# A pre-norm block with linear attention and an MLP: attention weights turned by DMA from DRAM, key folds by 128 rows, and a new hand-written order ahead of the MLP

## The chip, the cores and the metric

The kernel runs on one core of a Trainium2 chip. A core has five engines that run side by side, each with its own queue of instructions: TensorE (PE in the profile; PEld is its weight load), VectorE (DVE), ScalarE (ACT), GpSimd (POOL) and SyncE (SP), which here only issues DMAs. They wait for each other through semaphores. The metric is the device time of one execution in microseconds (us), as the median of several runs.

## What is computed

The reference, cut to what matters (x is 2048 tokens by D = 576, 32 heads of 18, F = 4608, all in bf16):

```python
def attention(x, wqkv, w_phi, wo):
    q, k, v = split(x @ wqkv)                     # 32 heads of 18
    pq, pk = q @ w_phi[head], k @ w_phi[head]
    phi = lambda p: concat(softmax(p), softmax(-p))
    kv = phi(pk).T @ v ; z = phi(pk).sum(tokens)
    o = (phi(pq) @ kv) / (phi(pq) @ z + 1e-6)
    return o @ wo
h   = x + attention(layernorm(x), ...)
y   = layernorm(layernorm(h))                     # one by the block, one by the MLP
out = h + gelu(y @ w1 + b1) @ w2 + b2
```

## The kernel before, in words

**Tiles.** The 2048 tokens lie in 16 tiles of 128, handled as 8 pairs p = 0 to 7 (a = 0 or 1 is the tile in the pair). `xh` holds x. D is cut into 9 chunks of 64. A normalised pair (`lnb`, three buffers in turn) is transposed into `lnT` so that partitions 0 to 63 hold a chunk of tile a = 0 and 64 to 127 the same chunk of tile a = 1. A projection (`project`, L420) is then 18 matmuls of 64 rows, two at a time on the two halves of TensorE, 9 chunks deep; every weight must therefore lie on both halves of the partitions.

**Attention weights.** The feature matrix `w_phi` is folded into the key and query weights once: `spread` (L215) lays `w_phi` out as a block diagonal `bd`, and a fold multiplies turned weights by it. For the keys, `load_wk` (L153) loads them in three DMAs, `flip_mm` (L361) turns them by 25 transposes on TensorE, `flip_ev` (L369) copies them out of PSUM, and `fold_k_mm` (L376) folds one chunk of 64 rows twice, once for either half of the partitions (10 matmuls, 9 chunks, 90 in all); `fold_k_ev` (L388) is the copy out of PSUM into `wkp`, all nine on ACT. For the queries, `load_wq` (L597) makes five DMAs in pieces of 252 bytes, `turn_wq` (L373) turns them by five DMAs from SBUF to SBUF, and five `fold_mm("q", c)` fold 128 rows each; `swap_q` (L409) copies halves across, so that query projections already read crossed slots of their weights (`CROSSED`, L418). The value weights are loaded to partitions 0 to 63 by two DMAs (`load_values`, L163) and copied to 64 to 127 by four GpSimd copies (`copy_values`, L171).

**Work of a pair.** `stats` (L287, VectorE), `power` (L298, GpSimd: variance to the power of -1/2), `centre` and `scale` (L305, L308: the normalised tile, on the engine named in the call), then the turning: `turn_x_mm` on TensorE for pairs 0 and 1, `turn_dma` (L320, issued by SP) for the others. Then for either half i of the heads `value_mm` and `key_mm` (TensorE into PSUM), `value_ev` (copy), `key_exp` (two exponentials on ACT), `key_sum` (L491: sum and reciprocal, VectorE), `key_weigh` (L494: the product with the reciprocal, one call for each a, all on GpSimd) and `sums(p, a)` (L554: 11 matmuls that gather phi(k) times v over all tokens in `acc_kv`). Queries: `query_mm`, `query_exp`, then `query_sum`, `query_weigh` and `turn_q` (a DMA transpose) when the pair's output is due. When all 16 `sums` are done, `table` (L569) takes `acc_kv` into `kvm`; `combine_mm`, `divide`, `turn_o_mm`, `residual_mm`, `residual_add`, `residual_stats`, `second`, `rescale` and `turn2_mm` carry pair 0 to the MLP's input, and the first matmul of the MLP is L1150. The MLP (`up` L1137, `down` L1178) runs over blocks of 256 or 512 tokens; attention outputs of later pairs are worked in between.

**Order.** The order on all engines is the order in which the calls stand (a manual schedule); L771 to L1116 are a list of some 340 calls, from `warm(13)` (TensorE matmuls on the identity) to `gelu_table()`. An engine takes its own instructions in that order and waits at each for what it needs. PSUM for this stage is three buffers of two banks (`two`), handed out in turn, and `pn`. The turned weights, `bd` and `wph` are borrowed from the space of the first quarter of the MLP's first weights (`borrowed`, L123), so `load_w1(0, n)` waits for the last fold that reads there; `load_w1(1, n)` waits until keys and values are given up (`close_keys`, L619).

## Time and profile before

| | us |
|---|---|
| median of 3 runs | 392.42 (392.41 to 392.46) |
| span of the profiled execution | 391.0 |
| first key fold on TensorE | 9.61 |
| first projection | 15.82 |
| first `combine_mm` | 71.03 |
| first matmul of the MLP | 85.26 |

The profile shows one execution. Its span runs from the first to the last instruction, and the runs' median lies 1.4 us above it. Rows of the timeline give start, duration, engine, line, operation, output <- inputs, shapes and count. Rows by line give busy time in us, the mean of one in ns, and the idle time ahead of them with what ended it. Rows by windows give a stretch and its length, then the busy time (and count) of PE, PEld, DVE, ACT and POOL, the granted TensorE clock, the share of the DMA engines and their GB/s. In a DMA row, "to landing" is the time from issue to the last byte.

### The profile page before, as it was taken

The page shows a single profiled execution, that of the slowest core. Times are in us where ns is not written, and L with a number is a line of the kernel's source. Part 1 is how long each engine was busy: PE and PEld are TensorE (multiplying, and loading weights), DVE is VectorE, ACT ScalarE, POOL GpSimd, SP SyncE. Part 2 cuts the span into 40 slices and gives each one's busy share as a digit, 9 for nine tenths or more (in the row PEclk, how much of TensorE's full clock was granted, in tenths as well). Part 3 has the DMA queues.
Part 4 walks back from the last instruction along what each step waited for, and adds up shares of the span by engine and source line. Part 5 has one row for each costly group of instructions (what it writes and reads, how often), then busy time and mean ns, then how long its engine had stood idle before and what let it go on. Part 6 is the DMA issues. An engine that isn't in the chain of part 4 may idle for free.

```text
span 391.0 us, 10251 instructions
## 1 busy us (share of the span) xinstructions
PE 383.6 (98%) x4492; PEld 267.2 (68%) x4493; DVE 163.5 (42%) x367; ACT 163.7 (42%) x290; POOL 128.2 (33%) x167
## 2 busy tenths in 40 slices
PE   8899999999999999999999999999999999999997
PEld 4687777779878887844457887444677764447773
DVE  6989894595249388590029322000480000000100
ACT  3978887678501850056650000666300026661000
POOL 8899999214604564144003111000031110000120
PEclk9999999999999999999999999999999999999999
DMA  8999749999655666643005542000041000000000
GB/s 220 189 182 175 163 98 184 227 300 254 206 106 104 95 107 134 107 61 62 0 2 63 90 106 48 16 1 2 2 102 50 17 17 0 2 2 0 17 29 18
DMA packets 76108, 34.76 MB, mean 89 GB/s; under 512 B 63026, under 2 KB 73536, under 8 KB 76064
## 3 DMA queue, kind: packets, MB, share of 16 engines
q1 hardware_dynamic: 75376, 32.47, 41.9%
q0 software_dynamic: 400, 1.35, 1.3%
q8 instruction: 35, 0.57, 0.6%
q10 hardware_dynamic: 288, 0.30, 0.3%
q14 instruction: 9, 0.07, 0.1%
HBM read 16.53 MB, written 2.36 MB: 48 GB/s over the span
## 4 chain that ended last, share of the span: by engine, by line
PE 94%; DVE 4%; POOL 1%; issue 1%; POOLq 0%
PE po L1194 36%; PE ph L1150 36%; PE pk L426 7%; PE pa L697 5%; PE pv L426 4%; PE acc_kv L562 2%; PE pw L250 1%; PE pn L648 1%; DVE st L293 1%; POOL wv L174 1%; DVE ob L662 0%; PE pW L396 0%; DVE shared L260 0%; PE pT L338 0%; DVE shared L314 0%
## 5 line engine op out<-in xcount | busy, mean ns | idle before, releaser
L1172 ACT ACTIVATE home<-ph,b1col 128x512 bf16<-128x512 f32 (+1 forms) x180 | 98.5, 598 | 169.6 <-PE ph L1150 166.3
L1194 PE MATMUL po<-w,home 128*128 128x288 bf16 (+2 forms) x1151 | 143.3, 286 | 0.1
L1150 PE MATMUL ph<-shared,w 64*128 64x512 bf16 (+2 forms) x1638 | 141.3, 332 | 0.1
L1194 PEld LDWEIGHTS <-home 128*128 128x128 bf16 x1152 | 109.2, 98 | 32.3 <-issue 1.8
L1150 PEld LDWEIGHTS <-w 64*128 64x128 bf16 x1638 | 80.3, 94 | 60.0 <-issue 1.0
L1198 DVE TENSOR_TENSOR ot<-po,hb 128x288 bf16<-128x288 f32 (+2 forms) x32 | 14.5, 454 | 106.5 <-PE po L1194 100.7
L1183 POOL TENSOR_TENSOR hb<-xh,b2bc 128x576 f32<-128x576 bf16 x16 | 20.4, 1272 | 104.6 <-DVE ot L1198 95.2
L426 PEld LDWEIGHTS <-home 64*128 64x128 bf16 x864 | 42.0, 94 | 10.8 <-issue 1.1
L512 POOL TENSOR_TENSOR padded<-home,rq 128x540 bf16<-128x540 bf16 x32 | 34.8, 1101 | 36.4 <-DVE rq L504 14.9
L256 POOL TENSOR_TENSOR rs<-va,mhalf 128x1 f32<-128x1 f32 x16 | 8.8, 550 | 105.0 <-DVE va L254 105.0
L706 DVE TENSOR_TENSOR xh<-pa,xh 128x288 bf16<-128x288 f32 x32 | 13.2, 449 | 71.6 <-PE pa L697 71.6
L483 POOL TENSOR_TENSOR phik<-phik,rk 128x576 bf16<-128x576 bf16 x32 | 36.4, 1164 | 1.4 <-PE pv L426 0.9
L477 DVE TENSOR_REDUCE sk<-phik 128x64 f32<-128x1152 bf16 x16 | 21.2, 1327 | 5.4 <-ACT phik L448 5.4
L448 ACT ACTIVATE home<-pk 128x576 bf16<-128x576 f32 x32 | 18.9, 649 | 6.9 <-PE pk L426 5.7
L503 DVE TENSOR_REDUCE sk<-home 128x64 f32<-128x1152 bf16 x16 | 21.0, 1313 | 0.0
L426 PE MATMUL pv<-wv,home 64*128 64x288 bf16 x288 | 20.9, 283 | 0.1
L426 PE MATMUL pk<-wqp,home 64*128 64x288 bf16 x288 | 20.0, 283 | 0.2 <-ACT home L448 0.2
L448 ACT ACTIVATE phik<-pk 128x576 bf16<-128x576 f32 x32 | 18.7, 652 | 3.1 <-PE pk L426 3.1
L426 PE MATMUL pk<-shared,home 64*128 64x288 bf16 x288 | 19.9, 283 | 0.0
L661 DVE RECIPROCAL rec<-pn 128x18 f32<-128x18 f32 (+1 forms) x32 | 8.0, 250 | 27.9 <-PE pn L648 27.9
L697 PE MATMUL pa<-wo,shared 64*128 64x288 bf16 x288 | 18.8, 283 | 0.0
L697 PEld LDWEIGHTS <-shared 64*128 64x128 bf16 x288 | 13.9, 94 | 4.3 <-issue 0.5
(78 smaller groups left out, 209.0 us busy)
## 6 DMA issues: line engine op xcount, KB each, us to landing
w<-in_B_w_dram SPq DMA_DIRECT2D x21, 432.0 KB, 7.0
out_dram<-ot SPq DMA_DIRECT2D x15, 144.0 KB, 1.9
xh<-in_A_x_dram SPq DMA_DIRECT2D x3, 576.0 KB, 7.3
wo<-in_A_wo_dram SPq DMA_DIRECT2D x4, 324.0 KB, 6.3
w<-in_B_w_dram POOLq DMA_DIRECT2D x3, 432.0 KB, 10.5
wv<-in_A_wqkv_dram SPq DMA_DIRECT2D x2, 324.0 KB, 9.9
w<-in_A_wqkv_dram SPq DMA_DIRECT2D x4, 157.5 KB, 8.7
wqp<-wqp SPq DMA_DIRECT2D x2, 288.0 KB, 3.9
```

Source lines behind the costliest of these rows:

```text
L426: nc.tensor.matmul(dst[:, a, 0:HALF], lhs[rows, c, :], w[rows, slot, i * HALF : (i + 1) * HALF], start=(n == 0), stop=(n == KC - 1),)
L448: nc.scalar.activation(rows[:, :, i * HH : (i + 1) * HH, s, :], flight[key, p, i][:, :, 0:HALF].rearrange("p a (h f) -> p a h f", f=DH), A ...
L477: nc.vector.tensor_reduce(sk[:, :, :], part_of(dst, i), AX.X, ALU.add)
L483: eng.tensor_tensor(part, part, flight["r" + key, p, i][:, a, :].rearrange("p (h o) -> p h o", o=1).to_broadcast([P, NH, DH]), ALU.mult,)
L503: nc.vector.tensor_reduce(sk[:, :, :], part_of(phiq[p], i), AX.X, ALU.add)
L512: eng.tensor_tensor(padded[:, a, g0 * P : (g0 + 5) * P].rearrange("p (g k) -> p g k", k=P)[:, :, 0:STEP].rearrange("p g (h f) -> p g h f", ...
L697: nc.tensor.matmul(pa[a], oT[p % 2][rows, c, :], wo[rows, c, cs], start=(c == 0), stop=(c == KC - 1),)
L1150: nc.tensor.matmul(ph[half][:, lo:hi], w1[p_ // 9][rows, c, p_ % 9 * P : (p_ % 9 + 1) * P], ln2T[rows, c, base + lo : base + hi], start=(c ...
L1172: nc.scalar.activation(hidden(m), ph[half][:, 0:width], AF.Gelu_apprx_tanh, bias=b1col[:, m : m + 1], scale=1.0,)
L1183: nc.gpsimd.tensor_tensor(hb[:, :], xh[:, t, :], b2bc[:, :], ALU.add)
L1194: nc.tensor.matmul(po[:, :], hidden(m)[:, i_ * P : (i_ + 1) * P], w2[m // 18][:, m % 18, cs], start=(j == 0), stop=(j == NM - 1),)
L1198: nc.vector.tensor_tensor(ot[:, cs], po[:, :], hb[:, cs], ALU.add)
```

## The change

- **Key and query weights** are turned by DMA straight from DRAM: ten `dma_start_transpose` of 576 rows by 128 columns (pieces of 256 bytes), five for the keys ahead of everything else on SP behind one load of x, five for the queries later in the order. `load_wk`, `flip_mm`, `flip_ev`, `load_wq` and the memsets of padding go.
- **Key folds** take 128 rows at once: 5 matmuls instead of 10 (the ninth still has 10). The weights then lie in slots that hold two neighbouring chunks, one on either half, so keys and values are read crossed like the queries (`WINDOWS`).
- **Value weights** come by four DMAs, whole rows, loaded for both halves; no copy on GpSimd.
- **x** is loaded in larger parts, the first parts from ACT's queue; tiles 12 to 15 ahead of 8 to 11.
- **b1** is turned by a DMA instead of a TensorE transpose.
- **Engines:** 8 of 16 `scale` calls are on GpSimd (none before), 4 on ACT (8 before), 4 on VectorE (8 before); 10 of 32 `key_weigh` and 1 of 4 `query_weigh` on VectorE (none before); 3 of 9 `fold_k_ev` on VectorE; one of the two last `turn2_ev` on ACT. Some memsets change between VectorE and GpSimd. Small tiles have other numbers of buffers.
- **Order:** a new list of calls; `load_w1(1, n)` is issued inside `close_keys`, still by SP and GpSimd in turn.

The diff of the helpers, cut:

```diff
+    def turn_weights(dst, at, g):
+        nc.sync.dma_start_transpose(
+            dst[:, g, :], A_wqkv[:, at + g * 126 : at + g * 126 + P]
+        )
+    def turn_wk(g):
+        turn_weights(wTk, D, g)
+    def turn_wq(g):
+        turn_weights(wTq, 0, g)
+    def load_values(part, eng):
+        if part < 2:
+            eng.dma_start(
+                wv[:, 4 * part : 4 * part + 4, :],
+                A_wqkv[part * KH : part * KH + 512, 2 * D : 3 * D].rearrange(
+                    "(c p) f -> p c f", p=P
+                ),
+            )
+            return
+        r0 = 512 if part == 2 else 0
+        eng.dma_start(
+            wv[(part - 2) * KH : (part - 1) * KH, 8, :], A_wqkv[r0 : r0 + KH, 2 * D : 3 * D]
+        )
...
+    load_x(0, 1, nc.scalar)
+    load_x(1, 2, nc.sync)
+    load_x(2, 4, nc.scalar)
+    load_x(4, 8, nc.scalar)
+    for g in range(NG):
+        turn_wk(g)
...
-    def fold_k_mm(c):
-        flight["k", c] = two.tile([P, 2, 512], FP32, name="pW", tag="two")[:, :, :]
+    def fold_k_mm(n):
+        flight["k", n] = two.tile([P, 2, 512], FP32, name="pW", tag="two")[:, :, :]
+        if n < 8:
+            f0 = n // 4 * KH + n % 4 * P
+            parts = [(slice(0, P), slice(f0, f0 + P))]
+        else:
+            parts = [(slice(0, KH), slice(512, D)), (slice(KH, P), slice(0, KH))]
         for g in range(NG):
             k = P if g < NG - 1 else 72
-            for a in range(2):
+            for rows, fs in parts:
                 nc.tensor.matmul(
-                    folded_part(g, "k", c, slice(a * KH, (a + 1) * KH)),
-                    wT[:k, g, c * KH : (c + 1) * KH],
+                    folded_part(g, "k", n, rows), wTk[:k, g, fs],
...
-    PLAIN = [(c, c) for c in range(KC)]
+    WINDOWS = [(n, (2 * n, 2 * n + 1)) for n in range(4)]
+    WINDOWS += [(4 + n, (2 * n + 1, 2 * n + 2)) for n in range(4)] + [(8, (8, 0))]
```

The new order as a whole (the list before has the same kinds of calls, with the differences named above), calls in a row:

```python
    warm(12); load_values(0, syn); stats(0, 0); load_values(1, pool); stats(0, 1); load_values(3, syn); power(0); centre(0, 0); stats(1, 0);
    scale(0, 1, vec); stats(1, 1); load_values(2, syn); spread(3); spread(4); stats(2, 0); scale(0, 0, act); spread(1); turn_x_mm(0); load_b1();
    spread(2); spread(0); load_x(12, 16, syn); power(1); turn_x_ev(0, 0, act); fold_k_mm(2); turn_x_ev(0, 1, act); fold_k_mm(1); fold_k_ev(1, act);
    fold_k_mm(4); fold_k_ev(2, dve); fold_k_mm(3); fold_k_mm(0); scale(1, 0, vec); fold_k_ev(3, dve); fold_k_ev(4, act); scale(1, 1, pool);
    load_x(8, 12, syn); fold_k_mm(6); stats(2, 1); fold_k_ev(0, act); turn_x_mm(1); fold_k_ev(6, act); fold_k_mm(7); turn_x_ev(1, 1, act);
    turn_x_ev(1, 0, dve); fold_k_ev(7, dve); fold_k_mm(8); turn_wq(3); power(2); stats(3, 0); fold_k_ev(8, act); stats(3, 1); fold_k_mm(5);
    value_mm(0, 1); fold_k_ev(5, act); stats(6, 0); turn_wq(1); key_mm(1, 0); centre(2, 1); power(3); value_mm(1, 1); scale(2, 0, pool); stats(6, 1);
    value_ev(0, 1, act); key_exp(1, 0); scale(2, 1, act); stats(4, 0); centre(3, 1); value_mm(1, 0); value_ev(1, 1, act); key_mm(0, 0);
    value_mm(0, 0); power(6); stats(4, 1); turn_wq(2); key_exp(0, 0); value_ev(1, 0, dve); value_ev(0, 0, act); turn_dma(2); scale(3, 1, act);
    stats(5, 0); scale(3, 0, pool); key_mm(0, 1); stats(5, 1); power(4); scale(4, 1, pool); key_sum(0, 0); value_mm(2, 0); turn_dma(3);
    key_exp(0, 1); power(5); key_sum(1, 0); key_sum(0, 1); key_mm(2, 1); key_mm(2, 0); value_ev(2, 0, act); key_weigh(0, 0, 1, pool);
    scale(5, 1, pool); key_mm(1, 1); key_exp(2, 1); key_exp(2, 0); scale(5, 0, pool); key_exp(1, 1); stats(7, 0); value_mm(2, 1); value_mm(3, 1);
    value_ev(2, 1, act); turn_wq(4); turn_wq(0); key_mm(3, 1); value_ev(3, 1, act); key_exp(3, 1); key_mm(3, 0); key_weigh(0, 1, 0, pool);
    scale(4, 0, vec); value_mm(3, 0); fold_mm("q", 0); key_weigh(0, 1, 1, pool); scale(6, 1, pool); key_sum(1, 1); stats(7, 1); turn_dma(4);
    key_sum(2, 1); key_weigh(1, 1, 1, pool); sums(0, 1); key_exp(3, 0); value_ev(3, 0, act); key_weigh(1, 0, 1, vec); fold_mm("q", 1);
    fold_ev("q", 0, act); power(7); key_weigh(1, 0, 0, vec); key_mm(4, 0); key_weigh(0, 0, 0, pool); key_sum(2, 0); fold_ev("q", 1, act);
    value_mm(4, 1); sums(0, 0); key_weigh(1, 1, 0, pool); key_exp(4, 0); value_ev(4, 1, act); fold_mm("q", 4); scale(6, 0, pool);
    fold_ev("q", 4, act); key_sum(3, 0); fold_mm("q", 2); fold_mm("q", 3); turn_b1(); fold_ev("q", 3, act); fold_ev("q", 2, act); sums(1, 0);
    turn_dma(5); sums(1, 1); key_mm(4, 1); key_exp(4, 1); centre(7, 0); scale(7, 0, act); key_sum(3, 1); key_mm(5, 0); value_mm(5, 0);
    key_weigh(2, 0, 0, pool); key_weigh(2, 1, 1, pool); key_exp(5, 0); load_wo(2); key_sum(4, 0); load_wo(1); value_ev(5, 0, act); swap_q(0);
    key_sum(5, 0); key_mm(5, 1); swap_q(2); value_mm(5, 1); window_masks(); scale(7, 1, vec); key_weigh(2, 1, 0, pool); swap_q(1); turn_dma(6);
    key_weigh(2, 0, 1, pool); key_exp(5, 1); query_mm(0, 1); value_ev(5, 1, act); query_mm(5, 0); query_exp(0, 1); query_exp(5, 0); value_mm(6, 1);
    load_w1(0, 4, syn); value_ev(6, 1, act); key_mm(6, 1); key_weigh(3, 0, 1, pool); query_mm(0, 0); key_sum(4, 1); value_mm(4, 0); key_exp(6, 1);
    query_exp(0, 0); key_weigh(4, 0, 1, vec); query_mm(3, 0); key_weigh(4, 0, 0, vec); value_ev(4, 0, act); key_weigh(3, 1, 0, pool); turn_dma(7);
    query_sum(0, 1); value_mm(7, 1); key_sum(5, 1); query_exp(3, 0); query_mm(4, 0); value_ev(7, 1, act); value_mm(7, 0); key_weigh(4, 1, 0, pool);
    key_mm(6, 0); key_sum(6, 1); key_weigh(3, 1, 1, pool); key_weigh(3, 0, 0, pool); query_exp(4, 0); query_sum(0, 0); key_weigh(4, 1, 1, vec);
    sums(3, 0); sums(2, 0); key_weigh(5, 0, 0, pool); sums(2, 1); key_mm(7, 1); key_weigh(6, 1, 0, pool); query_weigh(0, 1, 0, vec); key_exp(6, 0);
    value_ev(7, 0, act); key_sum(6, 0); key_mm(7, 0); query_mm(6, 0); key_exp(7, 1); query_weigh(0, 0, 0, pool); query_weigh(0, 1, 1, pool);
    key_weigh(6, 1, 1, pool); query_weigh(0, 0, 1, pool); query_mm(7, 0); load_w1(0, 0, syn); load_wo(3); load_w1(0, 5, syn); key_exp(7, 0);
    key_sum(7, 1); query_mm(2, 0); load_w1(0, 3, syn); key_sum(7, 0); key_weigh(5, 1, 1, vec); load_w1(0, 2, syn); key_weigh(5, 0, 1, pool);
    query_exp(6, 0); query_mm(7, 1); query_exp(7, 0); value_mm(6, 0); value_ev(6, 0, act); key_weigh(7, 1, 0, vec); sums(4, 0); load_wo(0);
    query_exp(7, 1); key_weigh(7, 1, 1, vec); key_weigh(5, 1, 0, pool); load_b2(); sums(5, 1); key_weigh(7, 0, 0, pool); key_weigh(7, 0, 1, pool);
    key_weigh(6, 0, 1, vec); sums(4, 1); sums(3, 1); key_weigh(6, 0, 0, vec); sums(7, 0); turn_q(0); query_exp(2, 0); sums(6, 1); sums(5, 0);
    sums(6, 0); sums(7, 1); query_mm(3, 1); table(0); load_w1(0, 1, syn); combine_mm(0, 0); query_exp(3, 1); copy_b1(act); combine_mm(1, 0, two);
    table(1); close_keys(); combine_mm(0, 1); divide(0); combine_mm(1, 1); divide(1); query_mm(1, 0); query_exp(1, 0); query_mm(4, 1); turn_o_mm();
    query_mm(5, 1); turn_o_ev(1, dve); turn_o_ev(0, dve); residual_mm(0, 1, double_bank()); residual_add(0, 1, 0); query_exp(4, 1);
    residual_add(0, 1, 1); residual_stats(0, 1, 0); query_exp(5, 1); residual_mm(0, 0, double_bank()); residual_add(0, 0, 0); query_mm(6, 1);
    residual_add(0, 0, 1); residual_stats(0, 0, 0); query_mm(1, 1); residual_stats(0, 0, 1); second(0); query_mm(2, 1); residual_stats(0, 1, 1);
    second(1); query_exp(6, 1); rescale(0, 1); query_exp(1, 1); rescale(0, 0); query_exp(2, 1); turn2_mm(0); rescale(1, 1); rescale(1, 0);
    turn2_ev(0, 1, dve); turn2_ev(0, 0, act); gelu_table(); load_w2(0, 0); load_w2(0, 1);
```

More of the change, by code (lines that the diff above doesn't have):

```diff
@@ new lines @@
+    scale(6, 1, pool)
+    key_sum(1, 1)
+    stats(7, 1)
+    turn_dma(4)
+    key_sum(2, 1)
+    key_weigh(1, 1, 1, pool)
+    sums(0, 1)
+    key_exp(3, 0)
+    value_ev(3, 0, act)
+    key_weigh(1, 0, 1, vec)
+    fold_mm("q", 1)
+    fold_ev("q", 0, act)
+    power(7)
+    key_weigh(1, 0, 0, vec)
+    key_mm(4, 0)
+    key_weigh(0, 0, 0, pool)
+    key_sum(2, 0)
+    fold_ev("q", 1, act)
+    value_mm(4, 1)
+    sums(0, 0)
+    key_weigh(1, 1, 0, pool)
+    key_exp(4, 0)
+    value_ev(4, 1, act)
```

673 lines of the change are left out of this document (292 added, 381 removed).

## Prediction

> **What bounds the kernel now.** I read the head of the page and its chain of work first: who holds the end?
>
> ```profile
> span 391.0 us, 10251 instructions
> PE 383.6 (98%) x4492; PEld 267.2 (68%) x4493; DVE 163.5 (42%) x367; ACT 163.7 (42%) x290; POOL 128.2 (33%) x167
> ...
> PE 94%; DVE 4%; POOL 1%; issue 1%; POOLq 0%
> ```
>
> TensorE (PE) is busy 98% of the span and makes 94% of the chain. The change edits only the order ahead of the MLP, so next comes the view by stages.
>
> ```profile
> 21.00:71.00 50.00, 50.00 (x866) 38.96 (x861) 39.19 (x61) 40.29 (x69) 45.96 (x52) 1.00 0.92 164
> 71.00:85.30 14.30, 13.22 (x216) 10.23 (x216) 10.45 (x29) 10.19 (x18) 2.61 (x5) 1.00 1.05 258
> 85.30:391.00 305.70, 302.92 (x3195) 206.50 (x3196) 97.03 (x230) 99.26 (x182) 61.73 (x72) 1.00 0.30 61
> ```
>
> From 85.3 us on PE is busy 302.9 of 305.7 us with work that the change does not touch, at a granted clock of 1.00. What can move is the 85.3 us before. Between 21 and 71 us PE has no gap at all; GpSimd (POOL) with 46.0 of 50 us is next. To see whether that busy PE is also dense, I take its timeline.
>
> ```profile
> 9.61 0.45 PE L381 MATMUL pW<-w 128*64 128x126 bf16 x10
> ...
> 15.82 2.38 PE L426 MATMUL pk<-shared,home 64*128 64x288 bf16 x36
> ...
> 63.74 1.27 PE L426 MATMUL pk<-wqp,home 64*128 64x288 bf16 x18
> 64.94 0.48 PE L562 MATMUL acc_kv<-vals,phik 128*128 128x57 bf16 x11
> 65.36 1.28 PE L426 MATMUL pk<-wqp,home 64*128 64x288 bf16 x18
> 66.47 1.26 PE L426 MATMUL pv<-wv,home 64*128 64x288 bf16 x18
> ...
> 68.77 1.11 PE L562 MATMUL acc_kv<-vals,phik 128*128 128x57 bf16 x33
> 69.82 1.28 PE L426 MATMUL pk<-wqp,home 64*128 64x288 bf16 x18
> ...
> 71.03 0.80 PE L648 MATMUL pn<-kvm,shared 128*128 128x57 bf16 x22
> ...
> 85.26 0.94 PE L1150 MATMUL ph<-shared,w 64*128 64x128 bf16 x27
> ```
>
> Start to start, a projection (18 matmuls) takes 1.11 us (65.36 to 66.47). One with a group of sums behind it takes 1.20 (63.74 to 64.94), the sums themselves 0.42 for 11 matmuls and 1.05 for 33. So 11 more sum matmuls cost 0.31, and each change from 64-row to 128-row matmuls and back costs about 0.2 (0.1 at either end). That gives three stretches: first key fold 9.61, first projection 15.82, first combine 71.03, MLP 85.26. The middle one holds 41 projections (45.3 us at 1.105), 16 sums (5.0), 5 query folds of five matmuls (about 0.27 each, 1.4), and some 13 changes of kind (2.8): 54.5 of its 55.2 us. PE is the bound there, and nothing else hides in it.
>
> **The change part by part.**
>
> Start. What releases the first fold and the folds after it:
>
> ```profile
> L389 ACT CAST shared<-pW 128x576 bf16<-128x576 f32 x9 | 5.1, 675 | 0.0
> L374 SPq DMA_TRANSPOSE w<-w x5: 1214/1253/1957, 20.0 to 28.2; - x5
> DMA to landing us min/median/max: 2.6/4.2/4.7
> L601 SPq DMA_DIRECT2D w<-in_A_wqkv_dram x5: 472/2030/3787, 6.6 to 16.0; - x5
> DMA to landing us min/median/max: 3.7/8.0/10.7
> 0.00:4.00 4.00, 2.58 (x7) 0.93 (x8) 2.66 (x9) 1.48 (x2) 3.00 (x13) 1.00 0.44 117
> 4.00:8.00 4.00, 4.00 (x23) 2.03 (x22) 1.57 (x7) 0.87 (x1) 3.16 (x11) 1.00 1.05 321
> 8.00:12.00 4.00, 3.46 (x73) 2.76 (x72) 3.93 (x13) 3.72 (x7) 3.76 (x7) 1.00 1.17 205
> 12.00:16.00 4.00, 2.56 (x53) 1.95 (x54) 3.86 (x13) 3.44 (x7) 3.31 (x7) 1.00 1.13 226
> ```
>
> The 25 flips on PE and their five copies go; instead every fold needs all five turnings from DRAM. SP issues them behind one x load, from about 1.4 us, at 1.25 us each, so the last starts at 6.4. A turning of data already in SBUF lands 2.6 to 4.7 us after issue; these weights' query loads from DRAM, in pieces of 252 bytes, took up to 10.7. So the last key rows land between 9.0 and 17.1; I take the turning's median, 10.6, since it is the same operation and size. First fold: 9.61 to 10.6, **+1.0**. Beside it POOL runs its five spreads, now behind memsets moved over from DVE and one DMA issue; I expect them to end ahead of the last turning, so they stay hidden.
>
> The pieces turned are 256 bytes. The Trainium skill, "DMA: Bandwidth & Descriptors", Specifications, wants at least 512 bytes per piece for line rate. That speaks against this edit, and the rows lean its way: 205 GB/s where the 252-byte loads run, 321 before them. By it, the 0.74 MB would take 3.6 instead of 2.3 us, an estimate, and the first fold would come at 11.9.
>
> The folds: nine evictions sat on ScalarE (ACT) alone, 5.1 us (0.56 apart), and made most of the 6.2 us from first fold to first projection. Now six are on ACT and three on DVE (DVE's price between 0.47 and 0.69 by rows below; I take 0.65), and the fold takes 50 matmuls instead of 90. Through three PSUM buffers I count: ACT's four first evictions end 3.2 us behind the first fold, the turning of x for pair 1 and the seventh fold follow, its eviction on DVE ends at 4.5, the first value projection starts at 4.6. **-1.6**, so the first projection comes at 15.2.
>
> That projection also needs all value weights. Bytes ahead of it, by the shapes: 8 tiles of x (1.18 MB), key weights (0.74), value weights twice (1.33), 3.25 MB. At the rates of the windows above (0.47 + 1.28 + 0.82 MB by 12 us, then 226 GB/s) that is reached at 15.0 us, a tie. The pieces are 1152 bytes instead of 576, which I leave as a reserve.
>
> Middle. The four POOL copies of the value weights go; ten key weighs of 32 and one query weigh move from POOL to DVE, eight scalings move to POOL. DVE's new load and the one price that no row has:
>
> ```profile
> L1198 DVE TENSOR_TENSOR ot<-po,hb 128x512 bf16<-128x512 f32 x1 | 0.7, 692 | 7.4 <-PE po L1194 7.4
> L293 DVE BATCH_NORM_STATS2 st<-xh 128x6 f32<-128x288 bf16 x32 | 12.6, 434 | 0.1
> L294 DVE BATCH_NORM_AGGREGATE mv<-st 128x2 f32<-128x12 f32 x16 | 3.3, 209 | 0.6
> L483 POOL TENSOR_TENSOR phik<-phik,rk 128x576 bf16<-128x576 bf16 x32 | 36.4, 1164 | 1.4 <-PE pv L426 0.9 <-DVE rk L479 0.4
> 29.03 10.20 POOL L483 TENSOR_TENSOR phik<-phik,rk 128x576 bf16<-128x576 bf16 x9
> 29.61 0.47 DVE L314 TENSOR_SCALAR shared<-xh,mv,rs 128x576 bf16<-128x576 bf16 x1
> 30.00 1.34 DVE L477 TENSOR_REDUCE sk<-phik 128x64 f32<-128x1152 bf16 x1
> ...
> 31.84 1.29 DVE L477 TENSOR_REDUCE sk<-phik 128x64 f32<-128x1152 bf16 x1
> ```
>
> A DVE weigh lies between DVE's cheapest pass over 576 elements (0.47) and what POOL pays for the same (1.16); the nearest row is DVE's own two-operand pass over 512 (0.69), so 0.65 from start to start. From the last DVE fold eviction (15.1) to the last weigh DVE then has 10 statistics at 0.98, 18 sums with reciprocal at 1.84 (30.00 to 31.84), 2 scalings, one value eviction, 11 weighs: 9.8 + 33.1 + 0.9 + 0.65 + 7.2 = 51.7, so it ends at 66.8, or some 67.6 with about 0.8 spent waiting for exponentials of keys 6 and 7. POOL gives up eleven weighs (12.8 us) and the copies and takes eight scalings (between 0.47, DVE's price, and 1.16; at 0.8 they are 6.4), so it has more room than before. PE comes to sums(6, 0), which wants DVE's last weigh, at 15.2 + 41 x 1.105 + 1.4 + 14 x 0.31 + 4 x 0.2 = 67.0. **DVE is as late as PE**: that cover is gone.
>
> The new order groups sums and folds into 4 blocks between projections instead of 13: nine changes of kind fewer, -1.9 us. One projection more (3, 1) stands ahead of the combine, +1.1. PE's own work is 42 x 1.105 + 5.0 + 1.4 + 0.9 = 53.7. Waits I put at 1.2: 0.6 for DVE's end, and 0.6 at value_mm(2, 0), the eighth projection, due at 22.9: its turn_dma(2) waits on SP for two statistics, a power and a scaling behind DVE's last fold eviction, near 18.7, and lands about 4.2 later, another tie. Behind it on SP stand turn_dma(3) and two query turnings; PE waits for those only five projections later, so only the first tie is priced. 54.9 instead of 55.2: **-0.3**, combine at 70.1. The projections read another slot of the weights, which costs nothing: queries, already crossed, and keys have the same pitch. SP's queue now has three query turnings ahead of turn_dma(2); the five 252-byte loads that held SP from 6.6 to past 16.0 are gone, which pays for them.
>
> Tail, combine to MLP:
>
> ```profile
> 79.74 0.46 DVE L706 TENSOR_TENSOR xh<-pa,xh 128x288 bf16<-128x288 f32 x1 [0.40 <-PE pa L697]
> 82.37 2.01 DVE L260 TENSOR_SCALAR shared<-xh,mv,rs 128x576 bf16<-128x576 bf16 x4
> 84.31 1.67 DVE L343 COPY shared<-pT 128x512 bf16<-128x512 bf16 x4
> L343 ACT COPY home<-pT 128x640 bf16<-128x640 bf16 x1 | 0.7, 692 | 0.0
> ```
>
> It is a chain through DVE, with seven query projections as filler; six remain. The second residual product follows the first at once, so DVE's second pair of adds starts at 78.9 instead of 79.74 (-0.85). One statistic slips behind second(0), +0.45. The last two evictions ran one behind the other on DVE (84.31 to 85.2); now one is on ACT beside it, 0.69 after the transposes, -0.4. **-0.8**, 13.4 instead of 14.2. Bias turning by DMA frees 0.2 us of PE that was filler anyway.
>
> Sum: 15.2 + 54.9 + 13.4 = 83.5 against 85.26, -1.7. What follows keeps its 305.7 us, as long as the second MLP weights land in time:
>
> ```profile
> 96.18 3.00 SPq L595 DMA_DIRECT2D w<-in_B_w_dram  x4
> 104.12 7.85 PE po L1194 x64
> 105.00:110.00 5.00, 5.00 (x43) 3.99 (x42) 1.95 (x6) 0.00 (x0) 0.00 (x0) 1.00 0.41 89
> ```
>
> The last four are issued by 99.2 and the DMA is slack after 105; the last piece is first read some 30 matmuls (0.123 each) into the second product, near 107.8. 1.7 us fit. The span becomes 389.3. The median of the runs, 392.42, lies 1.4 above the profiled span, so the forecast is **390.7 us**.
>
> **The rivals.** (1) The start is late: turnings or value weights land 1.7 us later than I took, inside 9.0 to 17.1. The 205 GB/s row speaks for it, the larger value pieces against. The gain is gone: 392.4. (2) DVE's weighs and POOL's weighs get in each other's way: both read two operands from SBUF, and no row of before has such a pair at once (all two-operand DVE rows read PSUM). If each DVE weigh waits out the running POOL weigh, half of 1.16 at 85% occupancy, 0.5 each, eleven cost 5.5; 1.4 of it fall into time in which DVE waits in the forecast anyway (0.8 for exponentials, 0.6 behind PE), and the combine comes 4.1 later: **394.8**, slower than before. It eats the whole gain from 0.28 us extra per weigh on (0.93 instead of 0.65). Against it speaks that the DVE scaling at 29.61 ran at 0.47 inside POOL's nine weighs, but it reads one tensor. The Trainium skill, "SBUF — State Buffer", Who interferes with whom, says that a DVE instruction with two SBUF inputs contends with a GpSimd one that reads SBUF, the loser fully blocked. By that rule this rival comes true; no run here shows it yet. (3) The change doesn't do what it says: the turning straight from DRAM goes in short pieces at the pace of the 252-byte loads, landing 8.0 (their median) instead of 4.2 after issue. First projection at 19.0, 3.8 later than forecast: 394.5.
>
> **How the numbers follow.** Forecast 0.50, rival (1) 0.17, rival (2) 0.28, rival (3) 0.05. A measurement of this kernel tells about 0.2% (0.8 us) from no change, so the forecast counts as faster (0.50), (1) as same (0.17), (2) and (3) as slower (0.33). Low end: no waits (-1.2) and a first projection at 14.1 (-1.1) give 388.4. High end: weighs at POOL's own price (1.16, or 0.5 more each) give 394.8, and with part of the late start on top, 1.2, 396.0. The forecast's own range is 388.4 to 391.6. Some 0.12 is left out.
>
> **What would show it.** Right: first projection near 15, a DVE weigh near 0.65, PE blocks of nine sums without a gap, combine near 70, MLP near 83.5, 305.7 after it. Wrong: DVE weighs near or above 0.9, or idle PE ahead of sums(6, 0); idle PE ahead of the first fold later than 11; a wait on turn_dma(2) above 1 us; PE gaps behind the MLP's start on the second weights.

## The result, and the profile after

The changed kernel takes 403.73 us (median of 4 runs, 403.53 to 407.91) against 392.44 for the kernel before in the same comparison: ratio 1.031, 95% interval 1.026 to 1.036. The forecast was 390.7, with a range to 396.0.

The head of the page and its chain of work, for the changed kernel:

```profile
span 402.0 us, 10091 instructions
PE 383.0 (95%) x4426; PEld 267.6 (67%) x4426; DVE 174.1 (43%) x368; ACT 158.8 (40%) x283; POOL 130.7 (33%) x159
...
PE 79%; DVE 12%; POOL 3%; issue 2%; DMA 1%; SPq 1%; ACT 0%; DVEq 0%; ACTq 0%
```

PE is busy as long as before (383.0 against 383.6 us); the span grew by 11.0 around it. The share of the chain that is not PE went from 6% to 21%: PE now waits. The view by stages, cut at the first projection, the first combine and the MLP:

```profile
18.19:83.21 65.02, 56.31 (x960) 44.14 (x958) 56.57 (x84) 43.17 (x75) 54.24 (x51) 0.97 0.73 122
83.21:96.08 12.87, 11.78 (x194) 9.05 (x195) 9.35 (x27) 8.94 (x17) 2.56 (x5) 1.00 1.01 264
96.08:402.00 305.92, 303.21 (x3198) 206.65 (x3196) 97.10 (x230) 99.76 (x182) 61.73 (x72) 1.00 0.29 61
```

Against before: first projection at 18.19 instead of 15.82 (+2.4), the middle 65.0 instead of 55.2 us (+9.8), the tail 12.9 instead of 14.2 (-1.4), the rest 305.9 instead of 305.7 (+0.2). That is the 11.0. PE's timeline shows where it stands:

```profile
10.58 0.48 PE L377 MATMUL pW<-w 128*128 128x126 bf16 x3 [0.92 <-POOL w L226]
12.04 0.29 PE L377 MATMUL pW<-w 128*128 128x126 bf16 x1 [0.98 <-DMA w<-in_A_wqkv_dram]
12.60 2.69 PE L377 MATMUL pW<-w 72*128 72x72 bf16 x26 [0.27 <-DMA w<-in_A_wqkv_dram]
...
18.19 1.36 PE L422 MATMUL pv<-wv,home 64*128 64x288 bf16 x18
...
39.44 0.34 PE L558 MATMUL acc_kv<-vals,phik 128*128 128x57 bf16 x6 [2.13 <-POOL phik L479]
...
45.54 0.61 PE L558 MATMUL acc_kv<-vals,phik 128*128 128x57 bf16 x11 [3.19 <-POOL phik L479]
46.08 1.76 PE L391 MATMUL pW<-w 128*64 128x126 bf16 x15
...
80.50 1.47 PE L558 MATMUL acc_kv<-vals,phik 128*128 128x57 bf16 x44 [1.97 <-DVE phik L479]
```

The number in brackets is idle time and what ended it. In the start PE waits for the spreads and then for the last key rows, until 12.6. In the middle it waits twice for POOL's key weighs (5.3 us) and at the end for DVE's (2.0). Behind the wait of 3.19, 15 fold matmuls took 1.76 us; the same 15 took 1.09 in the runs below where PE had not waited: the granted clock was 0.50 from 46 to 48 us. Who was slow? The groups of POOL and of DVE (busy us, mean ns of one, idle before):

```profile
L479 POOL TENSOR_TENSOR phik<-phik,rk 128x576 bf16<-128x576 bf16 x22 | 27.3, 1259 | 4.2 <-DVE rk L475 4.2
...
L320 POOL TENSOR_SCALAR shared<-xh,mv,rs 128x576 bf16<-128x576 bf16 x8 | 18.8, 2350 | 0.2
```

```profile
L473 DVE TENSOR_REDUCE sk<-phik 128x64 f32<-128x1152 bf16 x16 | 21.0, 1311 | 6.2 <-ACT phik L444 6.1
...
L479 DVE TENSOR_TENSOR phik<-phik,rk 128x576 bf16<-128x576 bf16 x10 | 11.2, 1167 | 0.0
...
L384 DVE CAST shared<-pW 128x576 bf16<-128x576 f32 x3 | 2.3, 756 | 3.8 <-PE pW L377 3.8
```

A scaling takes POOL 2.35 us, where the forecast had 0.8 and a bound of 1.16. A weigh takes DVE 1.17, where it had 0.65 and a rival at 1.16.

### The profile page after: what moved, and what is told of

It reads as the page before. It is cut to its first block, busy times and chain, and to the rows that moved or that the text cites. A ratio compares the mean times of both kernels' runs of the same rounds, so it can differ in the third digit from the quotient of the medians.

```text
span 402.0 us, 10091 instructions
## 1 busy us (share of the span) xinstructions
PE 383.0 (95%) x4426; PEld 267.6 (67%) x4426; DVE 174.1 (43%) x368; ACT 158.8 (40%) x283; POOL 130.7 (33%) x159
## 4 chain that ended last, share of the span: by engine, by line
PE 79%; DVE 12%; POOL 3%; issue 2%; DMA 1%; SPq 1%; ACT 0%; DVEq 0%; ACTq 0%
PE po L1156 35%; PE ph L1112 35%; PE pa L694 4%; DVE sk L473 3%; DVE phik L479 2%; DVE st L299 2%; DMA w<-in_A_wqkv_dram 1%; POOL shared L320 1%; SPq L155 1%; PE pn L645 1%; POOL phik L479 1%; DVE rk L475 1%; PE pk L422 1%; PE pW L377 1%; PE acc_kv L558 1%
## 5 line engine op out<-in xcount | busy, mean ns | idle before, releaser
L508 POOL TENSOR_TENSOR padded<-home,rq 128x540 bf16<-128x540 bf16 x31 | 34.5, 1127 | 35.6 <-DVE rq L500 18.7
L479 POOL TENSOR_TENSOR phik<-phik,rk 128x576 bf16<-128x576 bf16 x22 | 27.3, 1259 | 4.2 <-DVE rk L475 4.2
L444 ACT ACTIVATE phik<-pk 128x576 bf16<-128x576 f32 x32 | 18.7, 653 | 6.1 <-PE pk L422 5.5
L422 PE MATMUL pv<-wv,home 64*128 64x288 bf16 x288 | 20.0, 283 | 0.5 <-DMA home<-shared 0.5
L320 POOL TENSOR_SCALAR shared<-xh,mv,rs 128x576 bf16<-128x576 bf16 x8 | 18.8, 2350 | 0.2
```

What stands on the lines that cost most here:

```text
L320: eng.tensor_scalar(dst, src, mv[:, i, 0:1], rs[:, i : i + 1], ALU.subtract, ALU.mult)
L422: nc.tensor.matmul(dst[:, a, 0:HALF], lhs[rows, c, :], w[rows, slot, i * HALF : (i + 1) * HALF], start=(n == 0), stop=(n == KC - 1),)
L444: nc.scalar.activation(rows[:, :, i * HH : (i + 1) * HH, s, :], flight[key, p, i][:, :, 0:HALF].rearrange("p a (h f) -> p a h f", f=DH), A ...
L479: eng.tensor_tensor(part, part, flight["r" + key, p, i][:, a, :].rearrange("p (h o) -> p h o", o=1).to_broadcast([P, NH, DH]), ALU.mult,)
L508: eng.tensor_tensor(padded[:, a, g0 * P : (g0 + 5) * P].rearrange("p (g k) -> p g k", k=P)[:, :, 0:STEP].rearrange("p g (h f) -> p g h f", ...
```

## The experiments

Theory: POOL's scalings keep POOL from its weighs, and PE waits for those. Rivals: DVE's and POOL's weighs hold each other up; the start and the half clock behind it; the order of the list itself. Each section takes one of them.

### POOL's scalings

**On ACT instead** (in the changed kernel, all eight):

```diff
-    scale(1, 1, pool)
+    centre(1, 1)
+    scale(1, 1, act)
```

> The changed kernel, but the eight scalings that it has on GpSimd (POOL) are on ScalarE (ACT), each with its shift from POOL. Theory A (POOL's scalings at 2.29 us each hold up its weighs, and PE's sums wait for those): the POOL waits ahead of sums (2.1 and 3.2 us) and the clock dip behind them go, VectorE (DVE) loses its 6 us wait and bounds next; about 397 us, 6 to 7 below the changed kernel. Rival B (DVE and POOL block each other in the weighs and that is most of the loss): 401 to 402. Rival C (the late start at half clock is most of the loss): 402 or more.

Measured: 401.31 us, ratio to before 1.025 (1.021 to 1.029). PE's two waits for POOL are gone, but only 2.4 us came back. The wait moved. DVE's timeline, then PE's:

```profile
71.58 5.30 DVE L479 TENSOR_TENSOR phik<-phik,rk 128x576 bf16<-128x576 bf16 x5
```

```profile
76.27 2.24 PE L558 MATMUL acc_kv<-vals,phik 128*128 128x57 bf16 x44 [1.97 <-DVE phik L479]
79.93 0.80 PE L645 MATMUL pn<-kvm,shared 128*128 128x57 bf16 x22
```

DVE is busy without a gap from 36 to 76.9, and its last five weighs, 1.06 us each, are what PE waits for.

**The same scalings on POOL in the kernel before** (`scale(..., pool)` for the same eight):

> The kernel before, with only this changed: the eight scalings that the changed kernel has on POOL are on POOL. Theory A: POOL, busy for 64 of its first 68 us, gets 18 us more, its last weigh comes near 86 us, 407 to 410 us. By the price taken in the prediction (0.8 each, 6.4 in all): 397 to 398. If POOL's scalings are long only because VectorE blocks them: under 400.

Measured: 410.82, ratio 1.048 (1.046 to 1.049), so 18.8 us more. One line of that kernel, min/median/max of one:

```profile
L314 POOL TENSOR_SCALAR shared<-xh,mv,rs x8: 2282/2292/2297, 15.4 to 60.1; 128x576 bf16<-128x576 bf16 x8
```

Eight times 2.29 is 18.3: in the kernel before, where POOL is nearly full, nearly every us of it reaches the end. The price is POOL's own, since DVE has no weigh there to be in its way.

**What the price is made of** (the scalings of pairs 1 to 4 and of pairs 5 and 6 in two other forms):

```diff
+        elif eng is nc.gpsimd and p < 5:
+            eng.tensor_scalar(dst, src, mv[:, i, 0:1], None, ALU.subtract)
+        elif eng is nc.gpsimd:
+            eng.tensor_scalar(dst, src, 0.5, 0.25, ALU.subtract, ALU.mult)
```

> The changed kernel with its POOL scalings in other forms (their values are wrong in it): in pairs 1 to 4 one operation only (subtract the mean, an operand per partition), in pairs 5 and 6 two operations with constants instead of operands per partition. The full form took 2.29 us, POOL's product of two tensors of the same size 1.16. Theory (the pass pays for its second operation): one operation 1.1 to 1.3, two constants 2.3. Rival (it pays for the operands read per partition): one operation 1.7 or more, two constants 1.2. With half of the scalings shorter the time falls by 1 to 2 us from 403.7.

The rows of the two forms:

```profile
L320 POOL TENSOR_SCALAR shared<-xh,mv x4: 1730/1738/1743, 14.8 to 29.2; 128x576 bf16<-128x576 bf16 x4
```

```profile
L322 POOL TENSOR_SCALAR shared<-xh x4: 2137/2138/2147, 33.2 to 46.2; 128x576 bf16<-128x576 bf16 x4
```

Neither side: one operation costs 1.74, a second 0.4 to 0.55 more, and two operands per partition instead of constants 0.15. Even with one operation and one tensor to read it is dearer than the product of two tensors (1.16). The time, 401.69 from two runs, tells nothing: the profiled run began its projections late, at 21.1.

### Weighs on both engines

**The eleven weighs moved to DVE in the kernel before:**

```diff
-    key_weigh(1, 0, 1, pool)
+    key_weigh(1, 0, 1, vec)
...
-    query_weigh(0, 1, 0, pool)
+    query_weigh(0, 1, 0, vec)
```

> The kernel before with one part of the change alone: the same ten key weighs and one query weigh on DVE instead of POOL, at the places where they stand in the list before. Theory (DVE's and POOL's two-operand passes over SBUF hold each other up): DVE's weighs take 1.1 to 1.3 us in the mean with a fastest near 0.70, POOL's go from 1.16 to about 1.26; DVE gets 14 us of work instead of 7 and has about 6 us idle between 18.7 and 65 us to take it, so the combine comes 3 to 8 us later: 395 to 400. Rival (they do not interfere; the stretch seen after the change comes from something else): a weigh near 0.70 throughout, 7.5 us more on DVE, mostly in its idle time, and POOL relieved of 12.8: within 1 us of 392.4.

Measured: 395.31, ratio 1.008 (1.006 to 1.009), 3.2 us more. DVE's row has the stretch (fastest 0.69, slowest 1.71 us):

```profile
L483 DVE TENSOR_TENSOR phik<-phik,rk x10: 694/720/1711, 31.4 to 69.4; 128x576 bf16<-128x576 bf16 x10
```

PE's timeline, and then the windows (the last three columns are granted clock, DMA share, GB/s):

```profile
47.33 0.32 PE L562 MATMUL acc_kv<-vals,phik 128*128 128x57 bf16 x5
49.39 0.65 PE L562 MATMUL acc_kv<-vals,phik 128*128 128x57 bf16 x17 [1.74 <-DVE phik L483]
49.98 3.70 PE L426 MATMUL pk<-wqp,home 64*128 64x288 bf16 x36
```

```profile
48.00:50.00 2.00, 0.61 (x19) 0.57 (x21) 2.00 (x3) 1.01 (x2) 0.72 (x1) 1.00 0.65 148
50.00:52.00 2.00, 2.00 (x26) 1.42 (x26) 1.93 (x6) 0.45 (x1) 0.59 (x2) 0.71 0.03 8
52.00:54.00 2.00, 2.00 (x23) 1.17 (x20) 1.90 (x4) 1.03 (x3) 1.12 (x2) 0.50 0.00 0
```

Two DVE weighs, one of them beside a POOL weigh, made PE wait 1.74 us, and the wait cost nearly twice its length: the clock fell to half behind it, and two projections took 3.70 instead of 2.38. The Trainium skill, "TensorE: Matmul & The Clock Gate", Part 1, says that the clock halves after an idle window of about 3.4 us and comes back after a busy one. The length of the slow stretch fits (half from about 50.8 to 54.3); a wait of 1.74 was enough to start it, and there the measurement decides.

**The changed kernel with scalings on ACT and all weighs on POOL** (the first experiment, and `vec` becomes `pool` in ten key weighs and one query weigh):

> As e1_scale_act, and all key and query weighs of VectorE (DVE) go back to POOL, so that no DVE weigh runs beside one of POOL. Theory A: POOL gets 13 us more work, its first weigh starts near 30 us and 36 follow at 1.15, so it ends near 77 us and the time is 1 to 2 us above e1_scale_act (398 to 399). Rival B (blocking is most of the loss): 3 us or more below e1_scale_act.

Measured: 402.04, ratio 1.025 (1.023 to 1.027): no gain over 401.3. POOL's weighs are all back at 1.16, and PE waits for the last of those instead (1.54, 0.32 and 0.43 us in its sums).

**POOL's key weighs left out, scalings on ACT:**

> The changed kernel with its eight POOL scalings on ACT (as in the first experiment, 401.3) and with the 22 key weighs of POOL left out (those products are not computed; the ten key weighs on DVE and the query weighs stay). Theory (what is left of the loss in the middle is DVE's weighs held up by POOL's): each DVE key weigh takes 0.70 instead of a mean of 1.19, the five at the end take 3.2 instead of 5.3, DVE's chain ends 5 to 7 us earlier, the combine comes at 73 to 75 instead of 79.9, time near 395. Rival 1 (the list puts DVE's key sums late, the first at 25.2 instead of 18.7, and that alone sets the end): weighs get short but the combine stays at 77 or later, time above 398. Rival 2 (a DVE weigh is slow by itself): the weighs stay above 1.0.

Measured: 397.91, ratio 1.014 (1.012 to 1.016). DVE's row and timeline, then PE's:

```profile
L479 DVE TENSOR_TENSOR phik<-phik,rk x10: 694/744/755, 40.8 to 73.8; 128x576 bf16<-128x576 bf16 x10
```

```profile
71.16 3.36 DVE L479 TENSOR_TENSOR phik<-phik,rk 128x576 bf16<-128x576 bf16 x5
```

```profile
73.40 3.19 PE L558 MATMUL acc_kv<-vals,phik 128*128 128x57 bf16 x99
77.90 0.78 PE L645 MATMUL pn<-kvm,shared 128*128 128x57 bf16 x22
```

Without POOL's weighs beside it no DVE weigh takes more than 0.76, and PE's nine sums run in one piece. So the stretching is the neighbour's doing. The Trainium skill, "SBUF — State Buffer", Who interferes with whom, has this rule (a DVE instruction with two SBUF inputs against a GpSimd one that reads SBUF), and the runs agree: 0.70 alone, up to 1.72 beside a POOL weigh of 1.16, and POOL's up to 1.68. But from first projection (18.84 here) to combine there are still 59.1 us, where the kernel before has 55.2 and the first experiment 63.0. Contention explains at most half of what was left, since POOL's time for these weighs went with it: the weighs became as short as the theory had it, and the combine at 77.9 is as late as the first rival had it. Both are at work.

### The list

**The engine split of before in the changed kernel** (scalings on DVE, all weighs on POOL):

> The changed kernel with the engines as in the kernel before as far as they bear on this: the eight POOL scalings on DVE, all 32 key weighs and the query weighs on POOL. What is left of the change is the start, the list and the tail. Theory (beside the two engine moves the new list itself costs time, since its key sums begin on DVE behind 14 statistics and POOL's 32 weighs so begin late): 399 to 402, PE waiting for POOL's last weighs. Rival (with the engine split undone only the start's 2.4 us are left): 393.5 to 395.5.

Measured: 402.50, ratio 1.025 (1.023 to 1.027). That is 0.5 above the theory's range and far from the rival's: with no scaling on POOL and no weigh on DVE the kernel is hardly faster than the changed one.

**All key weighs left out, scalings on DVE:**

> The changed kernel with the eight POOL scalings on DVE and all 32 key weighs left out (those products are not computed); query weighs on POOL. Neither POOL nor the price of weighs can then hold TensorE. Theory (the rest of the middle's loss in the run without POOL's weighs, 59.1 us against 55.2, came from ACT carrying twelve scalings): from first projection to combine 54 to 56 us, as the forecast counted for TensorE's own work, time 392 to 394. Rival (the list itself leaves TensorE waiting for exponentials, copies and turnings): 58 or more, time above 396.

Measured: 395.26, ratio 1.007 (1.005 to 1.009), between the theory and its rival and nearer the theory.

```profile
17.53 1.28 PE L422 MATMUL pv<-wv,home 64*128 64x288 bf16 x18
...
37.74 1.27 PE L422 MATMUL pk<-shared,home 64*128 64x288 bf16 x18 [1.44 <-DMA home<-shared]
...
74.01 0.79 PE L645 MATMUL pn<-kvm,shared 128*128 128x57 bf16 x22
```

56.5 us from first projection to combine, with 2.1 of labelled waits: TensorE's own work is the 53.7 of the forecast within a us. The list has no fault on PE's side. It is the feeding of POOL: 56.5 without weighs, 64.0 with all of them on POOL (18.26 to 82.22 in the run before). Of these 7.5 us PE is idle for 3.3; for the other 4.2 it is busy longer with the same work (58.5 instead of 54.3 us, at a mean granted clock of 0.93 instead of 1.00). Part of that slow time lies in the start, as the first value projection there took 2.34 us instead of 1.28.

**Two attempts to feed POOL earlier**, both on that split. First the statistics, powers and scalings of pairs 5 and 6 behind the first key sums:

> The changed kernel with the engine split of before (402.5 us), and in addition the statistics, powers and scalings of pairs 5 and 6 moved from ahead of the first key sum to behind the key sums of pairs 0 to 2, so that the first key sum stands 3.9 us earlier in DVE's order (27.5 to about 23.5) and POOL's first weigh with it. Theory (the list's late key sums make POOL's 32 weighs end late, and TensorE waits for them): POOL's last weigh ends 2 to 4 us earlier, the combine with it, time 398.5 to 400.5. Rival (the key sums are late because their projections and exponentials are, or the pairs moved behind are then late themselves): DVE waits for exponentials in place of working, or TensorE for the turnings of pairs 5 and 6; 402 or more.

Measured: 405.54, ratio 1.035 (1.033 to 1.037), the wrong way. The first key sum came 2.0 us earlier, then held by its exponentials; POOL's powers of pairs 5 and 6 now stood between its weighs and waited 5.6 us for DVE's statistics. Then one sum and two weighs moved into time in which POOL idled:

```diff
+    key_sum(1, 0)
+    key_weigh(1, 0, 1, pool)
+    key_weigh(1, 0, 0, pool)
     stats(4, 0)
```

> The changed kernel with the engine split of before (402.5 us), with one key sum (pair 1, first half, whose exponentials are done by 23) moved ahead of the statistics of pair 4, and its two weighs on POOL behind it, ahead of the power of pair 4, where POOL idled. Theory (POOL begins its 32 weighs too late, at 29.5 instead of 22.1, and TensorE waits for its last ones): POOL's first weigh near 24.5, its last about 2 us earlier, combine and time 1.5 to 2.5 us earlier, 400 to 401. Rival (POOL's idle time for key sums between 30 and 40 merely grows, since DVE feeds it at its own pace): 402 to 403.5.

Measured: 399.00, ratio 1.015 (1.012 to 1.018), 3.5 us faster than the split alone. POOL's weighs in the two kernels, first the split alone:

```profile
L479 POOL TENSOR_TENSOR phik<-phik,rk x32: 1161/1165/1169, 29.5 to 77.8; 128x576 bf16<-128x576 bf16 x32
```

```profile
L479 POOL TENSOR_TENSOR phik<-phik,rk x32: 1154/1162/1166, 26.1 to 76.2; 128x576 bf16<-128x576 bf16 x32
```

In the kernel before the same 32 weighs run from 22.1 to 67.3. Three calls moved, nothing else changed, so part of POOL's lateness is shown to reach the end. Not all of it: the first weigh begins 3.4 us earlier, the last ends only 1.6 earlier, the combine comes 2.7 earlier (79.49 instead of 82.22). PE's wait of 2.46 for a POOL weigh at 43.4 is gone, and PE does its middle in 56.3 us instead of 58.5, since less of it runs at half clock. The new list has four value projections among its first six and the statistics of seven pairs, not five, ahead of the first key sum (25.6 us in the changed kernel, 18.7 before).

### The start

**Key weights turned from DRAM in the kernel before**, at the place of the three loads, without the flips:

```diff
-    load_wk(0)
-    load_wk(2)
-    flip_mm(3)
-    load_wk(1)
+    for g in range(NG):
+        turn_wk(g)
```

> The kernel before with one part of the change alone: the key weights come by five DMA turnings straight from DRAM, at the place of the three loads; the 25 flips on TensorE and their copies go; the folds stay as they were (90 matmuls, all evictions on ACT). Theory (turnings from DRAM land late and hold SP's queue): the last rows land near 12.5 as in the changed kernel, the first fold starts near 12.6 instead of 9.61, ACT's nine evictions follow behind it, the first projection comes near 18.5 to 19, and the time is 2 to 3 us longer, 394 to 395.5. Rival 1 (the forecast's step): landing 4.2 after issue, first fold at 10.6, first projection near 16.8, time 393.4. Rival 2 (the fold's start is not what sets the time, since the flips and their evictions went from PE and ACT): first projection within 0.5 of 15.8, no change.

Measured: 394.93, ratio 1.007 (1.006 to 1.009). Then the same with the loads of x for tiles 2 to 7 issued by ACT:

> The kernel before with the key weights turned from DRAM (394.9 us) and the loads of x for tiles 2 to 7 issued by ACT at the start instead of by SP behind the turnings. Theory (the turnings landed 4.1 after issue there because nothing shared the DMA engines with them; with x beside them they land 5 to 7.5 after issue as in the changed kernel): the last one lands near 12, the first fold comes near 10.5 to 12 instead of 8.9 with waits in it, the first projection at 17 to 18, time 393.5 to 394.5. Rival (x on the same queue was all that was wrong): landing stays near 4, the first projection comes at 15.8 or earlier, time 391 to 392.3.

Measured: 394.81, ratio 1.006 (1.004 to 1.007). Time to landing, min/median/max, and PE's folds in the one and in the other:

```profile
DMA to landing us min/median/max: 3.3/4.1/4.9
```

```profile
8.92 1.08 PE L375 MATMUL pW<-w 128*64 128x126 bf16 x20
12.44 3.74 PE L375 MATMUL pW<-w 128*64 128x126 bf16 x70 [2.44 <-DVE home L337]
```

```profile
DMA to landing us min/median/max: 4.0/5.8/8.0
```

```profile
10.85 4.73 PE L377 MATMUL pW<-w 128*64 128x126 bf16 x90 [2.06 <-POOL w L213]
```

With only ACT's two loads of x beside them, the turnings land 4.1 after issue, as the forecast took from the turning inside SBUF, and the first fold comes at 8.9. But then the rest of x stands behind them on SP: DVE waits for its tiles, and PE for DVE. With more of x beside them they take 5.8 (6.3 in the changed kernel). The small load of `w_phi` is late as well: the first fold now waits for the spreads, which wait for that load, until 10.9. Either way the time is the same.

**More matmuls on the identity in the start** (scalings on ACT; `warm(12)` becomes `warm(24)`, and `warm(14)` stands behind `turn_x_mm(0)`), against the half clock of the start (0.50 in the changed kernel from about 8.2 to 18.4 us, in the first experiment from about 10.8 to 17.4):

> As e1_scale_act, with 24 instead of 12 warming matmuls at the start and 14 more behind the first turning of x, which keep PE busy until the last key turning lands. If the half clock of 8 to 19 us costs time: the granted clock stays at 1.0, the first projection comes at 16.8 to 17.2 instead of 18.2, and the time is about 1 us below e1_scale_act. Rival: the stretch is bound by evictions and by VectorE's order, the clock stays up but the time is the same as e1_scale_act within 0.3 us.

Measured: 401.95, ratio 1.024 (1.022 to 1.026), against 401.31. The mean clock is 0.996, and nothing is gained: the first projection comes at 17.8 (16.9 in the first experiment), and PE then waits 2.6 us for two turnings of x. That it waited for DMAs in this start whatever its clock is the likely reason; it is not shown apart.

**The parts that only save work, in the kernel before** (folds by 128 rows from the flips, two copies on DVE, the new tail with the last query projection behind the transposes), and the same with each fold matmul issued twice:

> The kernel before with the parts of the change that save work and move none to another engine's neighbour: key folds by 128 rows from the flips as they were (50 matmuls instead of 90), two of nine fold copies on DVE, and the changed kernel's tail with the last query projection behind the transposes, so that it covers the last copies. Theory: ACT's nine copies set the fold's end, seven are 1.1 us less, so the first projection comes 0.8 to 1.2 earlier, and the tail is 0.7 shorter: 390.2 to 391.2. Rival (the copies on DVE push its statistics and the scaling of pair 1 back, and POOL's copies of the values set the first value projection anyway): 391.5 to 392.4.

> The kernel before with key folds by 128 rows, two of their nine copies on DVE and the changed tail (393.3 us), and each fold matmul issued twice into the same place, so that TensorE again has 90 of them in the start (the result is the same). Theory (the folds' missing matmuls leave TensorE idle so often that its clock falls to half, which stretched the first two projections from 2.38 to 3.74 us): granted clock 1.00 from 15 to 19 us, the two projections 2.4 us, time 391.8 to 392.3. Rival (the clock falls because of the wait ahead of the second turning of x, whatever the folds do): clock still 0.5 there, 393.3 or more.

Measured: 393.32, ratio 1.003 (1.002 to 1.004), and 393.29, ratio 1.003 (1.002 to 1.004). The first projections, in the one and in the other:

```profile
15.66 3.74 PE L432 MATMUL pk<-shared,home 64*128 64x288 bf16 x36
```

```profile
15.72 1.28 PE L432 MATMUL pk<-shared,home 64*128 64x288 bf16 x18
```

40 fold matmuls fewer brought the first projection only 0.2 us forward, and two projections then took 3.74 us at half clock; with the matmuls put back the clock is 1.00 and each takes the usual 1.28, as the theory had it. Still the time does not change: the combine comes at 70.94 instead of 71.40, but the tail behind it takes 15.1 us instead of 14.4, 0.68 of it in a wait for an exponential on ACT. Missing folds are not the whole cause of the half clock either: with all 90 folds, in the profiled run of the next section, the same two projections took 3.44 us, behind a wait of 1.15; in the kernel before a wait of 1.17 at the same place left the clock at 1.00. What decides it stays open.

### The tail

> The kernel before with the changed kernel's tail alone: the second residual product two calls behind the first, a statistic moved behind the second rescaling's start, one of the two last evictions on ACT. Theory (the tail is a chain through DVE and this order shortens it): combine at 71.03 as before, MLP 1.0 to 1.4 us earlier, time 391.0 to 391.4. Rival (the changed kernel's tail is shorter because it has six query projections in it instead of seven, not because of the order): seven projections still stand here, so no change, 392.4.

Measured: 392.02 against 392.16, ratio 1.000 (0.999 to 1.001). The new order alone, with its seven query projections:

```profile
71.32 0.80 PE L648 MATMUL pn<-kvm,shared 128*128 128x57 bf16 x22
...
85.52 4.67 PE L1150 MATMUL ph<-shared,w 64*128 64x128 bf16 x100 [0.75 <-ACT shared L343]
```

14.2 us, as before. DVE is done earlier, its last rescaling 12.2 us behind the combine instead of 13.35, the same 12.2 as in the changed kernel. But PE then still has its seven projections, and the copy on ACT stands behind two exponentials and holds the MLP for 0.75. The rival is right that the order alone returns nothing. The changed kernel has one projection fewer there (1.1 us, paid for ahead of the combine) and the order. That both are needed is argued, not shown: in the kernel before PE waited 0.28 us for DVE ahead of its last transposes, so with fewer projections and the old order DVE should set the end, but that was not run. No version that was run beats the kernel before.

## Why the prediction was wrong, step by step

- **First fold "9.61 to 10.6".** It came at 10.58, released by the spreads, which were not hidden as forecast; after three matmuls it waited for key rows until 12.60. The step "landing 4.2 after issue" holds for turnings with little beside them (4.1 measured); beside more of x the key turnings took 6.3 in the median, 7.5 at most.
- **"The folds: -1.6", first projection at 15.2.** It came at 18.19. The landing cost 2.0. The rest lies in matmuls at half clock, which the forecast did not count although it took work from PE, and in DVE copies at 0.76 instead of 0.65.
- **TensorE's own middle, 53.7.** Right: 56.5 with 2.1 of waits when nothing upstream holds it.
- **"POOL takes eight scalings, so it has more room than before".** This is the step that failed first. The bound of 1.16 was taken from another operation, a product of two tensors; the scaling took 2.35. 18.8 us instead of 6.4 on the engine that the view by stages had named next after PE. The rows had a POOL scaling of 128x2 and none of this size; the upper bound had no reason. The sum then had no term for PE waiting for POOL (its 1.2 us of waits were for DVE and for a turning), and PE waited 5.3 us for POOL's weighs.
- **And the step counted totals.** Even free of scalings POOL is late, since its first weigh comes at 26 to 30 instead of 22. Room ahead of the first weigh is no room. The list on POOL's side costs 7.5 us (56.5 against 64.0, waits and half clock together), shown by leaving the weighs out, and in part by feeding POOL earlier: 3.5 us, some of it in half clock that did not come.
- **Rival (2), weighs in each other's way.** Its price was right: 0.5 each forecast, 1.17 - 0.65 = 0.52 measured, and the query weigh 2.7 instead of 0.65. Its effect, 4.1 us later, is near the 3.2 measured with this part alone, but by luck: there only a few weighs were stretched (0.90 in the mean), and the 3.2 came from one wait and the half clock behind it, not from DVE's end. It was taken as an alternative to the forecast, and it is one cause among three.
- **DVE's end at 66.8.** It came at 81.1. In terms of the forecast's own sum: 2.4 for the later start, 6.7 for stretched weighs, 6.2 of waiting for exponentials (0.8 forecast, outside the 66.8), and about 1.0 less for the other rows. PE delivered those keys late because it waited for POOL: with PE's waits for POOL gone, in the first experiment, DVE's long wait (6.1 us up to 53.3) is gone too, and one of 2.0 at another place is left.
- **Tail -0.8.** It was -1.4. The chain through DVE and the six projections left were right in kind; DVE's part was 1.1, to the end of its rescaling, where 0.4 was forecast. The order alone gave nothing; it came with one query projection fewer, which the middle pays for.
- **MLP 305.7.** 305.9: right.

The causes do not add up. Scalings off POOL give back 2.4 us of 11.3; the split of before gives 1.2; without POOL's weighs 5.8, scalings on ACT; without any 8.5, scalings on DVE. These are differences of medians; against the kernel before in the same comparison they are 2.0, 0.9, 5.5 and 8.1. Each removal hands the end to the next late engine: POOL, then DVE, then POOL's weighs again, then the start. What stays open is how the start's 2.4 us divide between landing, half clock and the wait for the spreads; the first projection of the runs with this start lay between 16.9 and 21.1.

## What to carry to other kernels

Price a moved operation from a row of the same operation on the same engine; a row of another operation bounds nothing, and where there is none, the sum must be made for twice the dearest neighbour too. For each engine that is over 80% busy write down when it can begin and what it is fed by, not only how much it has to do. And where one removed wait returns little, look for the next engine in line before doubting the price.

## What the runs showed of the hardware that was not expected

- GpSimd's pass of one tensor with scalars is slower than its product of two tensors of the same size: 1.74 us with one operation, 2.14 with two constants, 2.29 with two operands per partition, against 1.16 (128x576, bf16). VectorE takes 0.47 to 0.57 for it.
- A TensorE wait of 1.74 us can cost 3: some 3.4 us at half clock behind it. But in the changed kernel waits of 2.13 and 1.97 left the clock at 1.00, and what decides is open. Work taken from TensorE ahead of other work can cost as well (two projections in 3.74 instead of 2.38 us), though a kernel with no work taken there showed it too (3.44).
- Five turnings from DRAM land 4.1 us after issue with little beside them and 5.8 to 6.3 beside more loads of x, at about 1.25 us of the issuing queue each, which is what made x late where it stood behind them.
